# A written list of TensorE's work units, attention groups whose parts may stand apart, and new durations in a kernel's planner

## The chip, the cores and the metric

The kernel runs on one core of one Trainium2 chip. The metric is the device time of one execution, in microseconds (us); the numbers quoted are medians over runs of the same program.

## The reference, cut to what matters

Gated linear attention feeds a gMLP block. B = 4 batches, H = 8 heads, S = 768 steps, D = 48; the model width is 384 and the hidden width 1024.

```python
for t in range(S):                                   # per batch and head
    state = alpha[t][:, None] * state + k[t][:, None] * v[t][None, :]
    y[t] = q[t] @ state
x = y, heads side by side                            # (B, S, 384)
u, v = split(gelu_tanh(x @ w_in))                    # each (B, S, 512)
v_n = (v - mean(v)) / sqrt(var(v) + 1e-6) * g_ln
v_s = einsum('ts,bsd->btd', w_sg, v_n) + b_sg[:, None]
out = x + (u * v_s) @ w_out
```

## The kernel before, in words

The sequence is cut into 24 chunks of 128 steps, numbered through: six for each of the four batches, three for each half of a batch. The recurrence is done chunk by chunk with decays folded into q and k. On VectorE each chunk takes two scans (`scan`, L334, and `recip`, L352), the products of q and k with the decays (`q`, L344, and `k`, L362), the masked scores (`causal`, L476), and three small updates of the running state (`half`, L496; `add`, L501; `state`, L504).

TensorE's work comes in units with short names, which the text uses throughout:

- A **group** serves two chunks at once: it closes chunk o and opens chunk i, and is written o.i (a dash where one is missing). It has three parts. G o.i (`squares`) holds the scores of chunk i, the first half of chunk o's output and the two gains of the state; M o.i (`squares_more`) the second half of o's output; H o.i (`squares_end`) the last reads of the state, which need VectorE's `half` of chunk o, and the transposes of chunk i's k. All but the transposes are small products that use the array in quarters (64 by 64). M waits for `turn` of chunk o (L455), a tiny copy on ScalarE that orders two halves of a bank.
- V b c (`mlp_v`) projects chunk c of batch b to the half that is normalised. Behind it stand gelu on ScalarE (L565), moments on VectorE (L569, L573), a root and a shift on GpSimd (L577, L582), the normalisation on VectorE (L589) or ScalarE (L585), and the split into a high part `vh` (ScalarE, L593) and a low part `vl` (VectorE, L597).
- U b h d (`mlp_u`) projects half h of a batch, column block d; ScalarE's gelu follows (L616).
- P b h d (`mlp_spatial`) multiplies all six v's of a batch with `w_sg`. Behind it stand a scale (VectorE, L631), the gate (VectorE or GpSimd, L636), and the split into `gh` (ScalarE, L641) and `gl` (VectorE, L646).
- R b h k (`mlp_out`) multiplies with `w_out`; VectorE adds x (L676) and the result is stored.
- Early on there are short products that make the low parts of the weights (`low_pe`, named wv, wu and ws with a number). The weights `w_out` (wo) and the second half of `w_sg` are split on ScalarE, VectorE and GpSimd.

Between the close of a chunk and the first V or U that reads it stands a chain: ScalarE copies the output (`xf`, L518, and `y3`, L508), six small DMAs pack it (L521), ScalarE makes the high part (`xh`, L529), and VectorE or GpSimd the low part (`xl`, L533).

A planner written in the kernel sets the order in which the instructions are emitted, and each engine executes its own in that order. `Plan.add` registers a step with an engine, a duration in ns, the steps it comes after, and the buffers it takes. `Plan.issue` keeps an estimated clock for each engine and emits, again and again, the step that could start first; among TensorE's steps within 150 ns of each other the one due earliest goes first. The due times come from `units`, a list of TensorE's work with durations, summed up from 5000 ns. A step of TensorE may go ahead of the list's first open unit by at most four places. Buffers are few: three banks of PSUM for the products of the MLP (`mm`), two tiles `vg`, two tiles `g`, one pair `gh` and `gl`, three tiles kqv.

Of the kernel before, what the change touches and what calls it, by code (L numbers as in the profile page):

```python
# [18 lines left out]
B, H, S, D = 4, 8, 768, 48  # L19
# [19 lines left out]


class Plan:
# [5 lines left out]
    RATE = 280.0  # L47

# [40 lines left out]
    def issue(self, units, ahead):  # L89
# [7 lines left out]
        port = [0.0, None]  # L97
        dma = 0.0
        while left:
# [3 lines left out]
            for n, s in left.items():  # L103
# [23 lines left out]
                for e, lock, ns, fn in s["ways"]:  # L127
                    t1 = max(t, free[e])
# [15 lines left out]
            fn()  # L144
            free[e] = end - {"dve": 75, "act": 100, "pool": 45}.get(e, 0)
# [17 lines left out]
def tile_gla_gmlp(ctx: ExitStack, tc: tile.TileContext, aT, kqv, w_in, w_sgT, w_out, g_ln, b_sg, out):  # L163
# [391 lines left out]
    def mlp_v(x, t, c):  # L555
# [39 lines left out]
        def low_half():  # L595
# [13 lines left out]
    def mlp_u(x, t, d):  # L609
# [43 lines left out]

    def mlp_out(g, x, b, hf, kk):
# [119 lines left out]


    def group(o, i):
        i = i if i is not None and i < n else None
        name = ("G", o, i)
        if o is not None:
            o_at[o] = name  # L780
        if i is not None:
            s_at[i] = name
        first = [(name, 95 + SLOT * (2 if o is None else 3 if i is None else 5))]
        if o is not None:
            first.append((("M", o, i), 2 * SLOT))
        return first + [(("H", o, i), (0 if o is None else SLOT) + (0 if i is None else 530))]
# [5 lines left out]
    def u(b, hf, d):  # L792
        return [(("U", b, hf, d), 1560)]

    def p(b, hf, d):
        return [(("P", b, hf, d), 3120)]

    def v(b, c):
        return [(("V", b, c), 2080)]

    def r(b, hf):
        return [(("R", b, hf, kk), 2080) for kk in range(NK)]

    units += v(0, 3) + u(0, 0, 0) + v(0, 4) + u(0, 0, 1) + v(0, 5) + p(0, 0, 0) + group(None, NCH) + u(0, 0, 2)
    units += p(0, 0, 1) + u(0, 0, 3) + p(0, 0, 2) + group(NCH, NCH + 1) + u(0, 1, 0) + p(0, 0, 3)
    for b in range(B):
        g = (b + 1) * NCH
        if b > 0:
            units += group(g - 1, g) + v(b, 3) + u(b, 0, 0) + u(b, 0, 1) + u(b, 0, 2) + u(b, 0, 3) + v(b, 4) + v(b, 5)
            units += u(b, 1, 0) + (group(g, g + 1) if b < B - 1 else [])  # L810
            units += p(b, 0, 0) + p(b, 0, 1) + u(b, 1, 1) + p(b, 0, 2) + u(b, 1, 2) + p(b, 0, 3) + u(b, 1, 3)
        else:
            units += u(b, 1, 1) + u(b, 1, 2) + u(b, 1, 3)
        if b < B - 1:
            units += group(g + 1, g + 2) + r(b, 0) + p(b, 1, 0) + group(g + 2, g + 3)
            units += p(b, 1, 1) + p(b, 1, 2) + p(b, 1, 3) + group(g + 3, g + 4) + r(b, 1)
            units += v(b + 1, 0) + v(b + 1, 1) + group(g + 4, g + 5) + v(b + 1, 2)
        else:
            units += p(b, 1, 0) + r(b, 0) + p(b, 1, 1) + p(b, 1, 2) + p(b, 1, 3)
            units += [(("R", b, 1, kk, "begin"), 1560) for kk in range(2)] + r(b, 1)  # L820
# [14 lines left out]
    for name, p in pieces:  # L835
# [107 lines left out]
    for name, ns in units:  # L943
        if name[0] == "G":
# [12 lines left out]
            plan.add(name, "pe", ns, lambda o=o, i=i: squares(o, i), deps, takes, due=due[name])  # L957
        elif name[0] == "M":
# [3 lines left out]
                due=due[name], keen=500,  # L962
# [206 lines left out]
```

## Time and profile before

| | us |
|---|---|
| median of 3 runs (374.67 to 375.32) | 375.32 |
| the profiled execution, its own time | 377.39 |
| its span, from the first to the last instruction | 375.7 |
| TensorE busy in it | 347.4 (92%) |
| VectorE busy | 266.1 (71%) |
| ScalarE busy | 152.8 (41%) |
| GpSimd busy | 60.4 (16%) |

A profile names the engines PE (TensorE), PEld (its weight loads), DVE (VectorE), ACT (ScalarE), POOL (GpSimd) and SP (the engine that issues the DMAs). A row of a timeline has the start and the length in us, the engine, the line of the kernel, the operation and its tiles; in square brackets stands the idle time of the engine before it and what ended that. A row of a table by stretches has the stretch, its length, then for each engine the busy time and in brackets the number of instructions, then TensorE's granted clock as a share of full speed, and what the DMA engines did. Matmuls overlap in the records, so that the duration of one (0.34 us for a product of 384 columns) is longer than the distance to the next.

### The profile page before, as it was taken

The page shows a single profiled execution, that of the slowest core. Times are in us where ns is not written, and L with a number is a line of the kernel's source. Part 1 is how long each engine was busy: PE and PEld are TensorE (multiplying, and loading weights), DVE is VectorE, ACT ScalarE, POOL GpSimd, SP SyncE. Part 2 cuts the span into 40 slices and gives each one's busy share as a digit, 9 for nine tenths or more (in the row PEclk, how much of TensorE's full clock was granted, in tenths as well). Part 3 has the DMA queues.
Part 4 walks back from the last instruction along what each step waited for, and adds up shares of the span by engine and source line. Part 5 has one row for each costly group of instructions (what it writes and reads, how often), then busy time and mean ns, then how long its engine had stood idle before and what let it go on. Part 6 is the DMA issues. An engine that isn't in the chain of part 4 may idle for free.

```text
span 375.7 us, 10732 instructions
## 1 busy us (share of the span) xinstructions
PE 347.4 (92%) x4492; PEld 316.7 (84%) x4492; DVE 266.1 (71%) x527; ACT 152.8 (41%) x367; POOL 60.4 (16%) x103
## 2 busy tenths in 40 slices
PE   2795989999998799999999999899999999999993
PEld 2564868799998688989999998799999989799993
DVE  4799987899996957897564986787376646443351
ACT  3385476755433333673222435543223336311010
POOL 1002123413201120320101211420111113300000
PEclk9999699999999989999999999999999999999999
DMA  8855575125246133432043335130212020000102
GB/s 307 279 192 156 197 236 190 42 73 189 83 139 220 31 110 119 142 93 77 6 156 113 111 81 184 47 118 29 91 66 90 9 69 10 1 2 0 63 4 68
DMA packets 18856, 39.38 MB, mean 105 GB/s; under 512 B 3952, under 2 KB 10992, under 8 KB 18800
## 3 DMA queue, kind: packets, MB, share of 16 engines
q1 hardware_dynamic: 18800, 38.61, 31.9%
q8 instruction: 37, 0.61, 0.7%
q14 instruction: 19, 0.16, 0.1%
HBM read 32.70 MB, written 4.72 MB: 100 GB/s over the span
## 4 chain that ended last, share of the span: by engine, by line
PE 64%; DVE 14%; DMA 7%; ACT 4%; issue 4%; SPq 3%; POOL 2%; DVEq 0%; ACTq 0%; POOLq 0%
PE mm_s L552 7%; PE mm_s L550 7%; PE mm_s L551 7%; DMA xf<-y 3%; PE mm_u L550 3%; PE mm_u L551 3%; PE mm_u L552 3%; DMA kqv_t<-in_kqv 3%; PE mm_o L552 3%; PE mm_o L551 3%; PE mm_o L550 3%; PE y L390 3%; PE mm_v L550 3%; SPq L521 3%; PE mm_o L666 3%
## 5 line engine op out<-in xcount | busy, mean ns | idle before, releaser
L550 PE MATMUL mm_s<-ws_hi,vh 128*128 128x384 f32 x192 | 66.0, 344 | 1.4 <-ACT ws_hi L224 0.8
L552 PE MATMUL mm_s<-ws_hi,vl 128*128 128x384 f32 x192 | 65.2, 339 | 0.1
L551 PE MATMUL mm_s<-ws_lo,vh 128*128 128x384 f32 x192 | 65.1, 339 | 0.2 <-DVE ws_lo L227 0.2
L641 ACT CAST gh<-g 128x384 fp32r<-128x384 f32 x32 | 16.3, 512 | 58.4 <-DVE g L636 40.5
L631 DVE SCALAR_TENSOR_TENSOR g<-mm_s,g_col,b_bc 128x384 f32<-128x384 f32 x32 | 19.5, 608 | 27.0 <-PE mm_s L552 26.9
L550 PEld LDWEIGHTS mm_s<-ws_hi,vh 128*128 128x128 f32 x192 | 36.0, 188 | 2.6 <-ACT ws_hi L224 1.1
L551 PEld LDWEIGHTS mm_s<-ws_lo,vh 128*128 128x128 f32 x192 | 36.1, 188 | 0.6 <-DVE ws_lo L227 0.4
L552 PEld LDWEIGHTS mm_s<-ws_hi,vl 128*128 128x128 f32 x192 | 36.0, 188 | 0.6 <-DVE vl L597 0.6
L377 PE MATMUL sc<-kqv_t 64*64 64x64 f32 x768 | 27.8, 231 | 7.2 <-DVE kqv_t L362 4.5
L550 PE MATMUL mm_u<-xh,wi_hi 128*128 128x384 f32 x96 | 33.1, 345 | 0.0
L377 PEld LDWEIGHTS sc<-kqv_t 64*64 64x64 f32 x768 | 25.5, 146 | 8.3 <-DVE kqv_t L362 4.9
L551 PE MATMUL mm_u<-xl,wi_hi 128*128 128x384 f32 x96 | 32.4, 338 | 0.0
L552 PE MATMUL mm_u<-xh,wi_lo 128*128 128x384 f32 x96 | 32.4, 338 | 0.0
L550 PE MATMUL mm_v<-wi_hi,xh 128*128 128x512 f32 x72 | 30.8, 428 | 1.4 <-ACT u L616 1.4
L334 DVE TENSOR_TENSOR_SCAN pf<-a,floor 128x516 f32<-128x516 f32 x24 | 30.0, 1251 | 2.1 <-DMA a<-in_aT 1.9
L352 DVE TENSOR_TENSOR_SCAN pf<-a,floor 128x516 f32<-128x516 f32 x24 | 29.5, 1229 | 1.1 <-ACT pend L340 0.4
L551 PE MATMUL mm_v<-wi_lo,xh 128*128 128x512 f32 x72 | 28.9, 401 | 0.0
L390 PE MATMUL y<-at,kqv_t 64*64 64x64 f32 x768 | 22.7, 234 | 6.7 <-ACT y L508 3.6
L390 PEld LDWEIGHTS y<-at,kqv_t 64*64 64x64 f32 x768 | 16.9, 141 | 14.2 <-issue 5.1
L552 PE MATMUL mm_v<-wi_hi,xl 128*128 128x512 f32 x72 | 28.7, 399 | 0.0
L569 DVE BATCH_NORM_STATS2 stats<-vg 128x6 f32<-128x512 f32 x24 | 16.5, 688 | 14.1 <-ACT vg L565 14.1
L552 PE MATMUL mm_o<-gh,wo_lo 128*128 128x384 f32 (+1 forms) x77 | 25.5, 331 | 0.0
(116 smaller groups left out, 801.6 us busy)
## 6 DMA issues: line engine op xcount, KB each, us to landing
kqv_t<-in_kqv SPq DMA_DIRECT2D x24, 768.0 KB, 4.3
a<-in_aT SPq DMA_DIRECT2D x24, 258.5 KB, 2.7
out_x<-r SPq DMA_DIRECT2D x23, 192.0 KB, 1.9
raw<-in_w_in SPq DMA_DIRECT2D x8, 384.0 KB, 5.5
xf<-y SPq DMA_DIRECT2D x144, 8.0 KB, 2.4
raw<-in_w_out SPq DMA_DIRECT2D x4, 384.0 KB, 3.1
raw<-in_w_sgT SPq DMA_DIRECT2D x6, 192.0 KB, 2.5
raw_sg<-in_w_sgT SPq DMA_DIRECT2D x1, 768.0 KB
```

Source lines behind the costliest of these rows:

```text
L334: nc.vector.tensor_tensor_scan(pf.rearrange("p j t -> p (j t)"), s["a"][:, 0:NP * C1], floor.rearrange("p j t -> p (j t)"), initial=0.0, o ...
L352: nc.vector.tensor_tensor_scan(s["pf"].rearrange("p j t -> p (j t)")[:, ::-1], s["a"][:, NP * C1:0:-1], floor.rearrange("p j t -> p (j t)" ...
L377: lambda j=j, h=h: nc.tensor.matmul(sc[half(h), e, 64 * j:64 * j + 64], k[half(e), j, half(h)], q[half(e), j, half(h)], start=True, stop=True,
L390: lambda j=j: nc.tensor.matmul(y_of(y, j, e)[:, half(h)], v[half(h), j, half(e)], at[half(h), e, j], start=first and j < 2, stop=True, ski ...
L521: nc.sync.dma_start(xf[64 * e + D:64 * e + 64, kk, tsl], y3[64 * e + 16 * kk:64 * e + 16 * kk + 16, :])
L550: nc.tensor.matmul(o, lh, rh, start=(idx == 0), stop=False)
L551: nc.tensor.matmul(o, lh, rl, start=False, stop=False)
L552: nc.tensor.matmul(o, ll, rh, start=False, stop=(idx == n - 1))
L569: nc.vector.bn_stats(t["stats"], t["vg"])
L631: nc.vector.scalar_tensor_tensor(t["g"], t["o"], g_col[:, d:d + 1], b_bc[:, tsl], op0=ALU.mult, op1=ALU.add,)
L641: nc.scalar.copy(g["h"][:, d], t["g"])
L666: nc.tensor.matmul(t["o"], lh[:, d, sl], g[rh][:, d], start=False, stop=(rh == "l"))
```

## The change

Three things change; the arithmetic and the instructions themselves stay.

1. The list `units` was computed by loops in the code, with each group's G, M and H next to each other. It is now read from a string `ORDER` with one token for each unit, in another order, where M or H need not follow right behind its G. `Plan.issue` treats the list as before, with the same four places of freedom.
2. Durations that the planner uses are changed, most of them upwards by 2 to 25%; for instance `("pe", 3120, product)` becomes `("pe", 3180, product)` for P, and GpSimd's root goes from 800 to 860.
3. The planner adds 50 ns to its estimate where TensorE goes from full products to those in quarters, and 110 ns for the way back.

Since the planner chooses at some steps between engines by its estimate, some work changes its engine as well. By the emitted order, seven of the 24 normalisations go from VectorE to ScalarE, three low parts of the second half of `w_sg` and two of the k products go from VectorE to GpSimd, one `xl` as well, and four gates and two additions for `w_out` go from GpSimd to VectorE.

```diff
+ORDER = """
+    H-.0 G0.1 M0.1 G-.0 G1.2 H1.2 M1.2 H0.1 G2.3 M2.3 V00 H2.3 H3.4 G3.4 U000 V01 M3.4 H4.5 G4.5 V02 G5.- M4.5 M5.-
...
+    RATE = 280.0
+    SWITCH = {("full", "tiled"): 50, ("tiled", "full"): 110}
...
-                    t1 = max(t, free[e])
+                    t1 = max(t, free[e] + (self.SWITCH.get((mode, s["mode"][0]), 0) if e == "pe" else 0))
...
-            ("pe", 2080, product), ("act", 600, gelu), ("dve", 665, moments), ("dve", 150, mean),
-            ("pool", 800, root), ("pool", 220, shift), (("dve*", 540, norm), ("act", 760, norm_act)), ("act", 615, high),
-            ("dve*", 665, low_half),
+            ("pe", 2100, product), ("act", 600, gelu), ("dve", 690, moments), ("dve", 175, mean),
+            ("pool", 860, root), ("pool", 270, shift), (("dve*", 545, norm), ("act", 810, norm_act)), ("act", 615, high),
+            ("dve*", 680, low_half),
...
-    for i in range(NCH):
-        units += group(i - 1 if i > 0 else None, i)
-        units.append((("V", 0, i - 3), 2080)) if i > 2 else None
-    units += group(NCH - 1, None)
...
+    def unit(token):
+        kind, rest = token[0], token[1:]
+        if kind in "GMH":
+            o, i = (None if x == "-" else int(x) for x in rest.split("."))
+            name = (kind, o, i)
...
+    units = [unit(token) for token in ORDER.split()]
```

What this does to the order is shown at three places. The buffers in the names carry numbers that differ between the two programs; the lines of the changed kernel are 17 higher from the attention on.

The first place is TensorE behind group 7.8, which closes chunk 7. Before, U 0 1 3 follows (`mm_u`):

```order
L400 MATMUL y_1450<-kqv_t_821,s_c_98 64x64 x8
L400 MATMUL y_1450<-kqv_t_821,s_m_100 64x64 x8
L471 MATMUL tp_1530<-ident_78,kqv_t_922 128x128 x4
L550 MATMUL mm_u_1536<-xh_767,wi_hi_103 128x384
L551 MATMUL mm_u_1536<-xl_804,wi_hi_103 128x384
L552 MATMUL mm_u_1536<-xh_767,wi_lo_104 128x384
```

Now P 0 1 2 follows there (`mm_s`):

```order
L417 MATMUL y_1501<-kqv_t_877,s_c_98 64x64 x8
L417 MATMUL y_1501<-kqv_t_877,s_m_100 64x64 x8
L488 MATMUL tp_1576<-ident_78,kqv_t_967 128x128 x4
L567 MATMUL mm_s_1585<-ws_hi_107,vh_859 128x384
L568 MATMUL mm_s_1585<-ws_lo_108,vh_859 128x384
L569 MATMUL mm_s_1585<-ws_hi_107,vl_882 128x384
```

U 0 1 3 has moved forward to just ahead of the H that opens chunk 6. Taken together, up to the H of group 8.9 TensorE's order has P 0 1 0 and P 0 1 2 where it had R 0 0 0; all other units ahead of that point are the same ones.

The second place is VectorE ahead of `half` of chunk 9 (the last row), which H of group 9.10 needs. Before, these rows lead up to it, of them the scales, gates and low parts of P 0 1 1, 0 1 2 and 0 1 3 (`g`, `gl`):

```order
L631 SCALAR_TENSOR_TENSOR g_1821<-mm_s_1770,g_col_109,b_bc_110 128x384
L348 RECIPROCAL floor_91<-pf_1798 128x4
L636 TENSOR_TENSOR g_1821<-g_1821,u_1442 128x384
L646 TENSOR_TENSOR gl_1827<-g_1789,gh_1800 128x384
L646 TENSOR_TENSOR gl_1827<-g_1821,gh_1800 128x384
L631 SCALAR_TENSOR_TENSOR g_1850<-mm_s_1802,g_col_109,b_bc_110 128x384
L636 TENSOR_TENSOR g_1850<-g_1850,u_1498 128x384
L646 TENSOR_TENSOR gl_1827<-g_1850,gh_1800 128x384
L631 SCALAR_TENSOR_TENSOR g_1898<-mm_s_1831,g_col_109,b_bc_110 128x384
L496 TENSOR_TENSOR s_m_100<-s_c_98,dl0_1857 128x4x48
```

Now these do; the row with `kqv_t_1768` is `q` of chunk 11, the one with `r_1822` the addition behind R 0 0 0:

```order
L518 TENSOR_TENSOR s_m_100<-s_m_100,sc_1667 128x4x48
L379 TENSOR_TENSOR kqv_t_1604<-kqv_t_1604,pf_1661 128x512
L693 TENSOR_TENSOR r_1782<-mm_o_1647,xf_280 128x384
L521 TENSOR_TENSOR s_c_98<-s_m_100,pend_97 128x4x48
L351 SCALAR_TENSOR_TENSOR pf_1786<-a_1642,floor_91 128x516
L365 RECIPROCAL floor_91<-pf_1786 128x4
L361 TENSOR_TENSOR kqv_t_1768<-kqv_t_1768,pf_1786 128x512
L693 TENSOR_TENSOR r_1822<-mm_o_1789,xf_280 128x384
L369 SCALAR_TENSOR_TENSOR pf_1786<-a_1642,floor_91 128x516
L663 TENSOR_TENSOR gl_1870<-g_1474,gh_1819 128x384
L513 TENSOR_TENSOR s_m_100<-s_c_98,dl0_1829 128x4x48
```

Between `half` of chunk 8 and `half` of chunk 9 stood 27 instructions and stand 15.

The third place is ScalarE around `turn` of chunk 2 (`alo2`) and the copy `y3` of chunk 2, which has to be done before G of group 3.4 may write its output. Before:

```order
L455 COPY alo2_102<-alo_89 128x1
L340 COPY pend_97<-pf_499 128x4
L484 COPY kn_548<-tp_538 128x512
L518 COPY xf_281<-y_457 128x3x128
L366 ACTIVATE a_345,low_96<-a_345,alo_89 128x4x128
L529 CAST xh_431<-xf_281 128x3x128
L508 COPY y3_567<-y_457 128x128
```

Now:

```order
L472 COPY alo2_102<-alo_89 128x1
L252 CAST ws_lo_108<-mm_w_435 128x384
L252 CAST ws_lo_108<-mm_w_442 128x384
L357 COPY pend_97<-pf_454 128x4
L281 CAST wi_hi_103<-top_525 128x384
L501 COPY kn_549<-tp_535 128x512
L535 COPY xf_280<-y_458 128x3x128
L281 CAST wi_hi_103<-top_540 128x384
L383 ACTIVATE a_383,low_96<-a_383,alo_89 128x4x128
L298 CAST wi_lo_104<-mm_w_564 128x384
L525 COPY y3_585<-y_458 128x128
L546 CAST xh_438<-xf_280 128x3x128
```

The copy `y3` has passed ahead of `xh` of chunk 1, and a weight product's copy (`wi_lo_104<-mm_w_564`) now stands ahead of it: the products wv 2 and wv 3 have moved on TensorE from behind group 3.4 to ahead of it. In TensorE's emitted order three groups stand apart: V 0 0 is between G and M of 3.4, U 0 0 0 between G and M of 4.5, and P 0 0 2, P 0 0 0 and U 0 1 3 between G and H of -.6. All other groups are emitted with their parts next to each other.

More of the change, by code (lines that the diff above doesn't have):

```diff
@@ L53, in add @@
         self, name, eng, ns, fn, after=(), takes=(), lead={}, due=None, soon=None, nbytes=0, other=None, keen=0,
-        start=0.0,
+        start=0.0, mode=("full", "full"),
     ):
@@ L60, in add @@
             name=name, eng=eng.rstrip("*"), ns=ns, after=list(after), takes=list(takes), lead=lead, due=due, soon=soon,
-            nbytes=nbytes, keen=keen, start=start, ways=[(e.rstrip("*"), e in ("dve*", "pool"), c, f) for e, c, f in ways],
+            nbytes=nbytes, keen=keen, start=start, mode=mode, ways=[(e.rstrip("*"), e in ("dve*", "pool"), c, f) for e, c, f in ways],
         )
@@ L97, in issue @@
         port = [0.0, None]
+        mode = "full"
         dma = 0.0
@@ L144, in issue @@
             fn()
+            if e == "pe":
+                mode = s["mode"][1]
             free[e] = end - {"dve": 75, "act": 100, "pool": 45}.get(e, 0)
@@ L791, in tile_gla_gmlp @@
-    units += group(NCH - 1, None)
[L792 to L820, printed above, removed]
+    def unit(token):
[3 more added lines that the diff above has]
+            name = (kind, o, i)
+            if kind == "G":
+                if o is not None:
+                    o_at[o] = name
+                if i is not None:
+                    s_at[i] = name
+                return name, SLOT * (2 if o is None else 3 if i is None else 5)
+            if kind == "M":
+                return name, 2 * SLOT
+            return name, (0 if o is None else SLOT) + (0 if i is None else 420 if o is None else 530)
+        if kind == "B":
+            return ("R", B - 1, 1, int(rest), "begin"), 1590
+        if kind == "C":
+            return ("R", B - 1, 1, NK - 1, 0), 0
+        return (kind, *map(int, rest)), {"U": 1590, "P": 3180, "V": 2100, "R": 2120}[kind]
@@ L864, in tile_gla_gmlp @@
         last = at("low_pe") if on_pe else at("low")
-        plan.add(at("size"), "act", 510, p["size"], [at("load")], takes=[("mag", 2, [last])])
-        plan.add(at("clamp"), "dve*", 330, p["clamp"], [at("size")])
-        plan.add(at("shift"), "dve*", 330, p["shift"], [at("clamp")], takes=[("top", 2, [last])])
+        plan.add(at("size"), "act", 550, p["size"], [at("load")], takes=[("mag", 2, [last])])
+        plan.add(at("clamp"), "dve*", 345, p["clamp"], [at("size")])
+        plan.add(at("shift"), "dve*", 350, p["shift"], [at("clamp")], takes=[("top", 2, [last])])
         plan.add(at("sign"), "dve*", 550, p["sign"], [at("shift")])
         plan.add(at("high"), "act", 510, p["high"], [at("sign")])
-        plan.add(at("power"), "dve*", 330, p["power"], [at("sign")])
+        plan.add(at("power"), "dve*", 345, p["power"], [at("sign")])
         plan.add(at("rest"), "dve*", 550, p["rest"], [at("power")])
@@ L956, in tile_gla_gmlp @@
             takes.append(("sc", 1, users))
-            plan.add(name, "pe", ns, lambda o=o, i=i: squares(o, i), deps, takes, due=due[name])
+            plan.add(name, "pe", ns, lambda o=o, i=i: squares(o, i), deps, takes, due=due[name], mode=("tiled", "tiled"))
         elif name[0] == "M":
@@ L970, in tile_gla_gmlp @@
                 name, "pe", ns, lambda o=o, i=i: squares_end(o, i), deps, takes, lead={last: 215}, due=due[name], keen=500,
+                mode=("full" if o is None else "tiled", "tiled" if i is None else "full"),
             )
@@ L1050, in tile_gla_gmlp @@
                     first = r + ("begin",)
-                    plan.add(first, "pe", 1560, begin, deps[:ND - 1], [("mm", 3, [r + ("add",)])], due=due[first])
-                    plan.add(r, "pe", 520, end, deps + [first], due=due[r])
+                    plan.add(first, "pe", 1590, begin, deps[:ND - 1], [("mm", 3, [r + ("add",)])], due=due[first])
+                    plan.add(r, "pe", 530, end, deps + [first], due=due[r])
                 elif (b, hf) == (B - 1, 1):
```

36 lines of the change are left out of this document (17 added, 19 removed).

## The prediction

> **What bounds the kernel now.** I read the page's head and its costliest group first, then the table by stretches, then the waits and timelines of the stretches in which TensorE (PE) loses time.
>
> ```profile
> span 375.7 us, 10732 instructions
> PE 347.4 (92%) x4492; PEld 316.7 (84%) x4492; DVE 266.1 (71%) x527; ACT 152.8 (41%) x367; POOL 60.4 (16%) x103
> L550 PE MATMUL mm_s<-ws_hi,vh 128*128 128x384 f32 x192 | 66.0, 344 | 1.4 <-ACT ws_hi L224 0.8
> 8.34:54.00 45.66, 37.17 (x752) 28.60 (x754) 41.09 (x83) 27.03 (x72) 5.91 (x6) 0.93 0.65 212
> 54.00:112.00 58.00, 56.89 (x731) 50.84 (x720) 52.77 (x113) 32.49 (x76) 15.56 (x21) 1.00 0.40 128
> 112.00:135.00 23.00, 19.08 (x213) 17.12 (x212) 17.32 (x32) 8.19 (x21) 3.12 (x3) 0.93 0.40 121
> 135.00:239.00 104.00, 104.00 (x1454) 96.87 (x1453) 76.72 (x149) 42.66 (x104) 17.74 (x33) 1.00 0.34 106
> 239.00:244.00 5.00, 3.58 (x16) 2.68 (x15) 3.54 (x6) 3.27 (x8) 1.70 (x2) 1.00 0.12 42
> 244.00:324.00 80.00, 80.00 (x1077) 75.28 (x1077) 49.70 (x102) 29.43 (x70) 12.48 (x24) 1.00 0.18 57
> 324.00:330.00 6.00, 5.34 (x30) 4.42 (x29) 3.47 (x8) 1.63 (x3) 2.16 (x4) 1.00 0.00 1
> 330.00:376.00 46.00, 39.85 (x235) 39.68 (x233) 16.89 (x31) 5.28 (x11) 0.00 (x0) 0.98 0.08 28
> ```
>
> The group at the top, the first of the three products of P, shows how long one matmul lasts (0.344). In the table, after each stretch's length stand the busy times of PE, its weight loads, VectorE (DVE), ScalarE (ACT) and GpSimd, then PE's clock. From 135 to 324 PE pauses in one place only, for 1.42. An order can win there next to nothing. Up to 54 PE is idle for 8.5 and from 112 to 135 for 3.9, and up to 112 DVE is busy 91% of the time: there DVE decides. The rest is PE's own work, the same before and after.
>
> **Prices of the units**, from places where PE doesn't wait: P, U, V, R, a whole group, and a P with a group right behind it.
>
> ```profile
> 249.18:252.36 3.18, 3.18 (x20) 3.18 (x20) 2.27 (x6) 1.31 (x4) 0.36 (x1) 1.00 0.44 170
> 255.53:257.12 1.59, 1.59 (x10) 1.59 (x10) 1.59 (x4) 0.57 (x2) 0.00 (x0) 1.00 0.28 69
> 319.00:321.10 2.10, 2.10 (x10) 1.70 (x10) 0.00 (x0) 0.49 (x1) 0.00 (x0) 1.00 0.00 0
> 271.31:273.39 2.08, 2.08 (x13) 2.08 (x13) 1.84 (x3) 0.00 (x0) 0.00 (x0) 1.00 0.07 12
> 265.15:267.58 2.43, 2.43 (x133) 2.36 (x133) 1.66 (x3) 0.70 (x2) 1.00 (x1) 1.00 0.03 7
> 261.88:265.15 3.27, 3.27 (x20) 3.02 (x19) 0.56 (x1) 0.76 (x2) 0.00 (x0) 1.00 0.00 0
> ```
>
> Going from full products to quarters costs 0.09 (3.27 against 3.18); a split group adds one such way there and back. Groups 3.4 and 4.5 are split (-.6 was left and entered once in either order): 2 x 2 x 0.09 = 0.4, in a stretch where PE waits for DVE, so I book nothing; uncovered, it is 0.4. The Trainium skill (TensorEngine Tiling, Tiling Modes) says that changing the mode drains TensorE. It speaks against splitting; the trace agrees that a change costs, with 0.09. The page gives no price; were each drain as long as a whole matmul, 0.344, the four changes would come to 1.4.
>
> DVE's prices are these means, and the next instruction starts some 0.07 before the one ahead has run out (110.92 + 0.34 against 111.19, further below).
>
> ```profile
> L352 DVE TENSOR_TENSOR_SCAN pf<-a,floor 128x516 f32<-128x516 f32 x24 | 29.5, 1229 | 1.1 <-ACT pend L340 0.4
> L631 DVE SCALAR_TENSOR_TENSOR g<-mm_s,g_col,b_bc 128x384 f32<-128x384 f32 x32 | 19.5, 608 | 27.0 <-PE mm_s L552 26.9
> L476 DVE TENSOR_TENSOR at<-sc,mask 128x512 f32<-128x512 f32 x24 | 16.3, 678 | 4.6 <-PE y L390 3.2 <-PE sc L377 1.3
> L597 DVE TENSOR_TENSOR vl<-vg,vh 128x512 fp32r<-128x512 f32 x24 | 16.1, 679 | 6.1 <-ACT vh L593 6.1
> L676 DVE TENSOR_TENSOR r<-mm_o,xf 128x384 f32<-128x384 f32 x23 | 12.4, 548 | 12.9 <-PE mm_o L666 12.4 <-DMA out_x<-r 0.4
> L533 DVE TENSOR_TENSOR xl<-xf,xh 128x384 fp32r<-128x384 f32 x17 | 9.4, 552 | 4.8 <-ACT xh L529 4.8
> L255 DVE TENSOR_SCALAR top<-mag 128x384 int32<-128x384 int32 x12 | 4.0, 351 | 0.0
> ```
>
> **Step 1, up to chunk 5.**
>
> ```profile
> 37.83 0.71 PE L390 MATMUL y<-at,kqv_t 64*64 64x64 f32 x16 [3.57 <-ACT y L508]
> 38.00:44.00 6.00, 6.00 (x137) 5.30 (x138) 6.00 (x12) 2.66 (x7) 1.44 (x1) 0.57 0.40 113
> 56.02 0.41 PE L400 MATMUL y<-kqv_t,s_m 64*64 64x64 f32 x16
> ```
>
> G 3.4 waits 3.57 for ACT's `y3`, which stood behind `xh`, and behind that idle time PE's clock is 0.57 for 6 us. The new order takes `y3` from behind `xh` and puts the products wv 2 and 3 into the gap, but these need their own DVE steps, which end some 5 us of work behind `half` of chunk 2 (a reversed scan, a q product, three like xl and five short ones); PE idles about as long as before and the clock falls as before. I book 0. The Trainium skill (TensorE: Matmul & The Clock Gate, Part 1) says that the clock halves after an idle window of about 3.4 us; the row agrees. By that rule a gap cut below it would save up to 2.6 (6.0 x 0.43) of PE time.
>
> The gain comes behind it. Ahead of H 5.- (56.02) PE's list gains product wu 0, U 0 0 0 and V 0 2: at least 1.59 + 2.10 + about 1.1 = 4.8. Ahead of DVE's `half` of chunk 5 five instructions leave (a scan, a k product, an xl, two tiny ones: 2.7) and twelve come (five like xl, two vl, one moments, four short: 6.0); less seven overlaps, +2.8. So H 5.- comes 2.8 later with 4.8 more done: PE is 2.0 better off.
>
> **Step 2, up to chunk 8.**
>
> ```profile
> 110.92 0.34 DVE L496 TENSOR_TENSOR s_m<-s_c,dl 128x192 f32<-128x192 f32 x1
> 111.19 1.23 DVE L352 TENSOR_TENSOR_SCAN pf<-a,floor 128x516 f32<-128x516 f32 x1
> 111.32 0.46 PE L400 MATMUL y<-kqv_t,s_m 64*64 64x64 f32 x16
> ```
>
> DVE's `half` of chunk 8 ends at 111.26 and H 8.9 starts at 111.32: DVE decides. Ahead of this `half` DVE has 199 instructions in either order; eleven are exchanged, nine of some 0.55 and two scales of 0.61 for ten of 0.55 and a tiny one, +0.5. Ahead of H 8.9 PE has P 0 1 0 and P 0 1 2 for R 0 0 0: 2 x 3.18 - 2.08 = 4.28 more. If DVE's idle time up to here stays, H 8.9 stands at 111.9, and PE is 3.7 better off (2.0 of it from step 1).
>
> **Step 3, group 9.10.**
>
> ```profile
> 120.90 0.69 DVE L344 TENSOR_TENSOR kqv_t<-kqv_t,pf 128x512 f32<-128x512 f32 x1 [2.90 <-DMA kqv_t<-in_kqv]
> 131.40 0.34 DVE L496 TENSOR_TENSOR s_m<-s_c,dl 128x192 f32<-128x192 f32 x1
> 130.51 0.46 PE L390 MATMUL y<-at,kqv_t 64*64 64x64 f32 x16 [2.26 <-ACT alo L455]
> 131.80 0.61 PE L400 MATMUL y<-kqv_t,s_m 64*64 64x64 f32 x16 [0.60 <-DVE s_m L496]
> 133.10:136.31 3.21, 3.21 (x11) 2.55 (x10) 1.18 (x3) 1.21 (x4) 0.00 (x0) 0.65 0.77 248
> ```
>
> M waits 2.26 for `turn` and H 0.60 for `half` of chunk 9, which is done 20.5 after that of chunk 8. V 1 0 then takes 3.21, not 2.10, at a clock of 0.65. Now 15 DVE instructions stand between the two halves: three scans or reversed scans would be 3.7, three additions 1.65, q, k and scores 2.1, a gl 0.58, five small 1.1, 9.1 in all and less overlaps 8.0. With `half` of chunk 8 at 111.3 + 0.5, that of chunk 9 ends at 120.1, or at 123.0 if the 2.90 for chunk 11's kqv come back whole (it is loaded once H 8.9 has freed its buffer, as before). PE reaches H 9.10 at 111.9 + 3.18 + 2.08 + 2.10 (P, R, V) + 2.43 = 121.7. I take 122.3, between the two, not 131.80: 9.5 earlier. V 1 0 is done by then and P 0 1 1 is not: 3.18 - 2.10 = 1.1 goes off. Of that H's own wait of 0.6 goes too, and V's slow clock (1.1). Together 10.1.
>
> **Step 4, the two later stalls, and what takes their place.**
>
> ```profile
> 243.01 0.50 PE L550 MATMUL mm_v<-wi_hi,xh 128*128 128x512 f32 x1 [1.42 <-ACT u L616]
> 324.98:329.44 4.46, 3.80 (x21) 3.16 (x20) 2.13 (x6) 1.14 (x3) 1.66 (x3) 1.00 0.01 2
> 230.23 0.66 PE L471 MATMUL tp<-ident,kqv_t 128*128 128x128 f32 x4
> 238.93 0.56 DVE L533 TENSOR_TENSOR xl<-xf,xh 128x384 fp32r<-128x384 f32 x1 [0.45 <-ACT xh L529]
> ```
>
> V 2 4 waited 1.42 behind a crowd of gelus; the new list spreads V's and U's, -1.4. P 3 0 0 takes 4.46 for 3.18 since the last `vl` is late; now U 3 0 3, U 3 0 0 and two R stand between V 3 4 and it (7.3 us), -1.2. New: U and V stand closer behind the chunks that they read. The chain for chunk 17 took 9.3 from its transposes (230.23) to the end of `xl` (239.49); V 2 2 now has 10, V 2 4 11, V 0 5 10 behind their chunks' H. Seven more normalisations on ACT lie in its 59% of idle time. These places cost between 0 and 6; I take 1.5, since most of the rows have a little to spare.
>
> Sum: 10.1 + 1.4 + 1.2 - 1.5 = 11.2. The profiled span of 375.7 becomes 364.5. The median lies 0.4 below that span: 364.1. The tail behind the last matmul keeps its order.
>
> **Rivals.** (a) A smaller gain: DVE's idle time up to chunk 9 grows by 3 to 8 (it had, by the two rows of the table that end at 112, 9.8 in all), or the new close reads take 5 to 6 and the idle time 1 to 4 more: 367.5 to 374.5. For it: every place in the new list has 0 to 2 us to spare; against: DVE has less work to do ahead of chunk 9. (b) Slower: DVE's `xl`, at the head of a queue that executes in order, waits for the packing DMAs.
>
> ```profile
> 60.32 0.56 DVE L533 TENSOR_TENSOR xl<-xf,xh 128x384 fp32r<-128x384 f32 x1 [1.20 <-ACT xh L529]
> ```
>
> Chunk 4's waits 1.20 before. Four such (chunks 1, 3, 4, 5) stand in DVE's new order up to V 0 5. Everything behind is moved by each us waited; from 2.8 more for each the gain is gone, and at 4 the time is 380. Against it: each stands behind 9 to 11 us of other work. (c) The list doesn't matter, since DVE's total hardly changes and it stays the bound up to the second batch: within 0.2%. Against it: DVE is busy 17.32 of 23.00 from 112 to 135. (d) More gain: the clock doesn't fall at 38 and no close read waits: 357 to 360.
>
> **How the numbers follow.** 0.2%, 0.75 us, is about what a measurement tells from no change. Forecast (360 to 367.5) 0.56, (a) 0.25, (b) 0.08, (c) 0.04, (d) 0.07. Faster is the first, (a) and (d): 0.88; same 0.04; slower 0.08. The range leaves out (b), (c), the slowest fifth of (a) and the lower half of (d), 0.2 in all: 358.5 to 372.5. It takes in the bounds of step 3 (H 9.10 from 121.7 to 123.3) and of step 4 (0 to 6).
>
> **What would show it.** H 8.9 near 112 and H 9.10 near 122 in PE's timeline; no wait of M 9.10 for `alo`; PE without pauses from 125 on, but for waits under 1 us at V 2 2, V 2 4 and V 3 5; P 3 0 0 in 3.2. The forecast is wrong if H 8.9 comes after 115, if DVE waits over 2 us for `xh` in the first 70 us, or if PE loses over 5 us behind 135.

## The result, and the profile after

The changed kernel takes 368.1 us (median; 365.55 to 370.98), the kernel before 375.2 on the same chips. The ratio is 0.986, with a 95% interval of 0.983 to 0.989; it leaves out executions of the kernel before that stood over 1.5% above its fastest (the profiled one, with 377.39, stood there too), and so gives 5.2 us (375.2 x 0.0139) where the medians give 7.1. The forecast was 364.1 and a gain of 11.2: the direction is right and the time lies in the range, but the gain is only 0.47 (by the ratio) to 0.63 (by the medians) of what was forecast.

The page's head and the table by the same stretches as before, of the profiled execution of after (367.87 us):

```profile
span 366.1 us, 10776 instructions
PE 343.3 (94%) x4492; PEld 315.0 (86%) x4492; DVE 263.3 (72%) x520; ACT 157.7 (43%) x374; POOL 61.3 (17%) x103
8.34:54.00 45.66, 38.56 (x747) 28.87 (x748) 38.87 (x82) 28.66 (x73) 4.71 (x8) 0.96 0.67 215
54.00:112.00 58.00, 56.62 (x614) 51.21 (x614) 53.85 (x110) 33.33 (x78) 17.15 (x20) 1.00 0.42 130
112.00:135.00 23.00, 21.55 (x472) 20.25 (x472) 21.38 (x40) 10.64 (x29) 7.80 (x9) 1.00 0.46 138
135.00:239.00 104.00, 104.00 (x1334) 97.21 (x1333) 78.43 (x153) 47.88 (x113) 21.49 (x36) 1.00 0.34 104
239.00:244.00 5.00, 5.00 (x95) 4.75 (x96) 2.43 (x5) 0.70 (x2) 0.00 (x0) 1.00 0.00 0
244.00:324.00 80.00, 80.00 (x1028) 75.83 (x1020) 49.25 (x99) 28.74 (x68) 8.50 (x19) 1.00 0.17 53
324.00:330.00 6.00, 6.00 (x36) 6.00 (x35) 3.20 (x6) 0.98 (x2) 0.00 (x0) 1.00 0.01 3
330.00:366.10 36.10, 30.09 (x180) 29.64 (x178) 11.30 (x22) 3.94 (x8) 0.00 (x0) 0.96 0.10 35
```

Behind 135 us PE no longer pauses until its last work is done: both late stalls are gone, and no close read put another in their place. From 112 to 135 PE is busy 21.55 of 23.00 (19.08 before). Up to 112 little changed, and DVE is still the fuller engine there. The timeline around the two places on which the forecast hung:

```profile
114.94 0.34 DVE L513 TENSOR_TENSOR s_m<-s_c,dl 128x192 f32<-128x192 f32 x1
115.33 0.29 PE L417 MATMUL y<-kqv_t,s_m 64*64 64x64 f32 x4 [1.45 <-DVE s_m L513]
121.02 0.69 DVE L361 TENSOR_TENSOR kqv_t<-kqv_t,pf 128x512 f32<-128x512 f32 x1 [0.52 <-DMA kqv_t<-in_kqv]
124.69 0.35 DVE L513 TENSOR_TENSOR s_m<-s_c,dl 128x192 f32<-128x192 f32 x1 [0.83 <-PE dl L428]
125.39 0.30 PE L417 MATMUL y<-kqv_t,s_m 64*64 64x64 f32 x8
```

DVE's `half` of chunk 8 begins 4.0 later than before (114.94 against 110.92), and PE, in H 8.9, waits 1.45 for it: H 8.9 comes behind 115, which the prediction named as a sign that it is wrong. `half` of chunk 9 then comes 9.75 behind it, not 20.5, and the wait for `alo` is gone.

To set whole executions side by side, I took for each of PE's units the time to the start of the next one, less the usual time of its kind (the 20th percentile over this case's profiles), and summed these losses by where the unit starts. The span less the loss is 339.6 to 340.1 in every row, so the work is the same and the loss is what differs. The first four rows are the two kernels, each with a second profile; the others are the experiments below (us):

```
                          0-60  60-115  115-140  140-end   all    span
before                   20.23    4.30     5.44     5.95  35.92  375.68
before, second profile   20.44    4.30     2.87     5.90  33.51  373.11
after                    18.60    4.03     0.55     2.97  26.16  366.08
after, second profile    18.65    3.62     0.92     2.85  26.05  366.19
list_alone               20.21    4.12     2.63     4.56  31.52  371.22
durations_alone          24.39    3.62     2.62     5.08  35.72  375.41
no_switch                16.72    6.85     6.54     3.62  33.73  373.78
groups_whole             22.58    7.20     4.52     5.88  40.18  379.92
list_to_H89              17.37    3.88     0.46     5.31  27.03  366.85
list_from_batch1         25.95    4.05     3.74    11.68  45.42  385.31
pool_one_input_before    19.96    3.63     3.03     4.89  31.51  371.49
pool_one_input_after     17.64    1.59     0.51     2.90  22.65  362.37
lows_on_vector           17.09    4.35     0.57     2.95  24.97  364.62
after_q_first            19.60    3.58     1.61     4.61  29.40  369.20
no_switch_q_first        15.67    7.00     5.72     3.00  31.38  371.05
before_q_first           19.89    5.04     0.95     4.54  30.42  370.18
```

### The profile page after: what moved, and what is told of

The parts are those of the page before. It is cut to its first block, busy times and chain, and to the rows that moved or that the text cites. A ratio compares the mean times of both kernels' runs of the same rounds, so it can differ in the third digit from the quotient of the medians.

```text
span 366.1 us, 10776 instructions
## 1 busy us (share of the span) xinstructions
PE 343.3 (94%) x4492; PEld 315.0 (86%) x4492; DVE 263.3 (72%) x520; ACT 157.7 (43%) x374; POOL 61.3 (17%) x103
## 4 chain that ended last, share of the span: by engine, by line
PE 77%; DVE 12%; issue 3%; DMA 2%; POOL 2%; ACT 2%; SPq 0%; DVEq 0%; ACTq 0%; POOLq 0%
PE mm_s L567 8%; PE mm_s L569 8%; PE mm_s L568 8%; PE mm_v L567 4%; PE mm_v L569 4%; PE mm_v L568 4%; PE mm_u L567 4%; PE mm_u L568 4%; PE mm_u L569 4%; PE y L407 3%; PE mm_o L569 3%; PE mm_o L568 3%; PE mm_o L567 3%; PE mm_o L683 3%; PE tp L488 3%
## 5 line engine op out<-in xcount | busy, mean ns | idle before, releaser
L567 PE MATMUL mm_v<-wi_hi,xh 128*128 128x512 f32 x72 | 29.8, 414 | 0.0
L594 POOL TENSOR_SCALAR rstd<-mv 128x1 f32<-128x1 f32 x24 | 8.3, 345 | 128.0 <-DVE mv L590 116.8
L693 DVE TENSOR_TENSOR r<-mm_o,xf 128x384 f32<-128x384 f32 x23 | 12.6, 550 | 21.2 <-PE mm_o L683 21.0
L567 PE MATMUL mm_o<-gh,wo_hi 128*128 128x384 f32 (+1 forms) x77 | 25.6, 333 | 0.0
L568 PE MATMUL mm_o<-gl,wo_hi 128*128 128x384 f32 (+1 forms) x77 | 25.6, 332 | 0.0
```

What stands on the lines that cost most here:

```text
L567: nc.tensor.matmul(o, lh, rh, start=(idx == 0), stop=False)
L568: nc.tensor.matmul(o, lh, rl, start=False, stop=False)
L693: nc.vector.tensor_tensor(t["r"], t["o"], x["xf"][:, kk], op=ALU.add)
```

## The experiments

The kernel before ran beside each set of experiments, with medians from 372.7 to 375.2 us. Medians of different sets therefore differ by up to 2.5 us without a cause in the kernel; the ratios, each to the kernel before of its own set, are what compares.

**Which part of the change carries it.** Four kernels took parts of it.

*list_alone* is the kernel before with the written list alone; *durations_alone* is the changed kernel with the old list:

```diff
 list_alone:       before.py, the loops over group, u, p, v, r replaced by
+    units = [unit(token) for token in ORDER.split()]
 durations_alone:  after.py, with the old loops back in place of that line
```

> The kernel before with the new list of TensorE's units, and the old durations and no price for a change of tiling in the planner. Theory: the list carries the gain, since the rows that got better are TensorE's (the group 9.10 without its wait for alo, no stall behind 125 us); 366 to 370 us, ratio to the kernel before 0.98 to 0.99. Rival: the corrected durations set VectorE's order, and VectorE is what TensorE waits for ahead of 115 us, so the list alone gains less than half: 372 to 375 us.

> The changed kernel with the old list, so that only the planner's durations and its price for a change of tiling differ from the kernel before. Theory (the list carries the gain): 373 to 377 us, within 0.5% of the kernel before. Rival (the durations carry it, by VectorE's order): 369 to 372 us.

Measured: 371.4 us for the list alone (ratio 0.995, 0.991 to 0.998) and 378.7 for the durations alone (1.010, 1.004 to 1.015). Neither theory holds, nor does a rival. The two parts add up to nothing (-3.8 and +3.5 by medians), together they give -7.1. In the timeline of durations_alone a place where it loses shows, and in the table of its stretches from 32 us on:

```profile
40.39 0.49 PE L407 MATMUL y<-at,kqv_t 64*64 64x64 f32 x8 [6.56 <-ACT y L525]
32.00:36.00 4.00, 1.57 (x56) 1.13 (x48) 4.00 (x10) 1.19 (x4) 0.00 (x0) 0.93 0.29 77
36.00:40.00 4.00, 0.00 (x0) 0.00 (x0) 4.00 (x11) 2.25 (x6) 0.16 (x1) 0.50 0.72 254
40.00:44.00 4.00, 3.61 (x128) 3.50 (x128) 4.00 (x7) 1.34 (x5) 0.92 (x1) 0.50 0.05 10
```

With the corrected durations the planner hands DVE other work first, and G 3.4 waits 6.56 us, not 3.57, with PE's clock at half speed behind it. The list puts two weight products and, further on, V 0 0 between a group's parts into this stretch; in the changed kernel no wait there is longer than 2.18. The list alone, with the old durations, already brings `half` of chunk 9 close behind that of chunk 8 (116.64), and M 9.10 and H 9.10 don't wait:

```profile
126.37 0.35 DVE L509 TENSOR_TENSOR s_m<-s_c,dl 128x192 f32<-128x192 f32 x1 [0.34 <-PE dl L424]
```

*list_to_H89* and *list_from_batch1* split the list in two:

```diff
 list_to_H89:       after.py
+    cut = ORDER.split().index("V10")
+    units = units[:cut] + [x for x in old if x[0] not in taken]
 list_from_batch1:  the old order through batch 0's R, then ORDER's rows for the rest
```

> The changed kernel with the new list up to the third row that holds R000 (through group 8.9's opening), and the old order of the rest; durations as in the changed kernel. By the two traces H 8.9 came only some 0.3 us better than before, so that the theory (the gain up to there was lost to VectorE, and comes only from group 9.10 on) gives 373 to 376 us. Rival (what is gained is already there at H 8.9, and the old order would keep it): 369 to 372 us.

> The changed kernel with the old list through batch 0's products R, and the new order for all that follows. In the two profiled executions 4.3 us of the 9.6 were gained behind H 9.10. Theory: the new order behind there takes the stalls of V24 and P300 away in every execution: 370 to 372 us. Rival: these 4 us were mostly one unlucky execution of the kernel before (its profiled time stood 2.2 us above its median), and the gain lies ahead of 125 us: 373 to 376 us.

Measured: 369.9 us (ratio 0.989, 0.983 to 0.995) for the head, against the theory and with its rival; 384.5 (1.026, 1.019 to 1.033) for the tail, which neither expected. The head with the old order behind it already has a loss of 0.46 from 115 to 140: there it doesn't matter what the list says behind H 8.9. It has lost 5.31 behind 140, like before (5.95), and P 3 0 0 takes 4.18 again:

```profile
316.38:320.56 4.18, 3.81 (x21) 3.17 (x20) 2.02 (x5) 1.73 (x4) 1.31 (x3) 1.00 0.01 2
```

So the new tail is worth the other 2.3 of the profile, and 1.8 of the medians, a difference that lies inside the interval. The tail behind the old head says nothing on its own worth: at the seam P 1 0 2 has to wait 2.58, and 5.7 us more than before are lost behind 140 (in an execution 2.5 above this kernel's median).

**Parts of a group apart.** In *groups_whole* PE takes nothing else between a group's G and its H:

```diff
+                if opened and s["ways"][0][0] == "pe":
+                    if n[1:] != opened or n[0] not in ("M", "H"):
+                        continue
```

> The changed kernel with one rule more in the planner: between a group's G and its H TensorE takes nothing else, so that a group's three parts stand together as before. Theory: the parts that stand apart hide the wait of M for alo (2.26 us in the group 9.10 before) and of H for half (0.6 us each in several groups of before); without them the groups 3.4, 4.5, 8.9 and some later ones wait again: 370 to 374 us. Rival: the durations already order VectorE and ScalarE so that these waits are short, and TensorE waits as long in sum wherever the parts stand: 367 to 369 us.

Measured: 377.6 us, ratio 1.009 (1.005 to 1.013): 9.5 above the changed kernel (8.5 by the ratios), past the theory's own end. The profiled execution was 4 us above this median, so its rows give places, not sizes. At M 4.5, behind whose G the changed kernel does U 0 0 0, PE stands first; later R waits for a low part of `w_out`, and DVE's q of chunk 11 for its load:

```profile
55.87 0.26 PE L422 MATMUL y<-kqv_t,s_c 64*64 64x64 f32 x1 [4.02 <-issue]
114.08 0.69 PE L574 MATMUL mm_o<-gh,wo_lo 128*128 128x384 f32 x1 [2.58 <-DVE wo_lo L310]
51.00:56.00 5.00, 0.98 (x63) 0.84 (x58) 2.92 (x10) 0.51 (x1) 2.57 (x6) 0.89 0.47 165
56.00:60.00 4.00, 4.00 (x30) 3.88 (x30) 2.85 (x6) 2.20 (x6) 0.00 (x0) 0.50 0.59 191
129.66 0.69 DVE L366 TENSOR_TENSOR kqv_t<-kqv_t,pf 128x512 f32<-128x512 f32 x1 [3.80 <-DMA kqv_t<-in_kqv]
```

At M 4.5 PE does 0.98 us of work in five, and its clock then halves. The loss from 60 to 140 is 11.7, against 4.6 in the changed kernel. But the waits that the theory names don't show: up to 140 us no M waits for `alo` and no H for `half` by more than 0.1, and the row of the longest wait names no releaser. So the time is shown and the cause isn't. The list was found for parts that may stand apart, so this is what it loses without them, not what another list for whole groups would take.

**Why `half` of chunk 8 came late.** DVE's idle time from 18 us to this instruction had grown by only 1.1 (7.6 against 6.5). Its instructions were longer: set against the median of their own kind, they were stretched by 6.0 in sum, against 2.9 before, and every stretched one lies beside a large two-input operation of GpSimd, of which there are 11 in that time, and 8 before. The 1.1 of idle time and 3.1 more of stretch account for the 4.0. From the timeline of after, ahead of `half`, with one more stretched row (0.35 is usual):

```profile
111.90 1.30 POOL L550 TENSOR_TENSOR xl<-xf,xh 128x384 fp32r<-128x384 f32 x1 [7.72 <-ACT xh L546]
112.32 1.29 DVE L653 TENSOR_TENSOR g<-g,u 128x384 f32<-128x384 f32 x1
113.16 1.30 POOL L653 TENSOR_TENSOR g<-g,u 128x384 f32<-128x384 f32 x1
113.54 1.48 DVE L361 TENSOR_TENSOR kqv_t<-kqv_t,pf 128x512 f32<-128x512 f32 x1
90.95 1.05 DVE L272 TENSOR_SCALAR top<-mag 128x384 int32<-128x384 int32 x1
```

DVE's gate takes 1.29, usually 0.56, and its q product 1.48, usually 0.69; they end 0.41 and 0.56 after GpSimd's operations (113.20, 114.46), as if most of each had begun only then. The Trainium skill (SBUF — State Buffer, Who interferes with whom) says that a DVE instruction with two SBUF inputs contends with a GpSimd instruction that reads SBUF, for a pair of ports that is an exclusive lock. The gate and the q product agree. The row at 90.95 has one tensor input and is stretched too (GpSimd works from 90.79 to 91.79), so two inputs aren't the whole condition. *pool_one_input_after* and *pool_one_input_before* make GpSimd's operations shorter and change no order; they leave one input out of the arithmetic:

```diff
-        eng.tensor_tensor(xl[:, :, tsl], xf[:, :, tsl], xh[:, :, tsl].bitcast(F32), op=ALU.subtract)
+        if eng is nc.gpsimd:
+            eng.tensor_copy(xl[:, :, tsl], xh[:, :, tsl].bitcast(F32))
+        else: ...            # and so for ws_lo, wo_lo, top, the gates and k
```

> The changed kernel with each large two-input operation of GpSimd (xl, the low halves of the spatial and output weights, the gates that GpSimd takes, k) made a copy of one of its inputs, the one that comes last; order and waits as they were, results not the reference's. Theory: ten VectorE instructions stretched by 0.2 to 0.8 us (6.0 us in sum up to half 8) each lie beside such an operation of GpSimd, which holds VectorE off by its second input; as copies they don't, the stretch sum falls below 1.5 us, H 8.9 comes at 110 to 112.5 us instead of 115.3, and the time is 363.5 to 366.5 us. Rival: any large operation of GpSimd holds VectorE so: stretch sum above 3 us, 367 to 369 us.

> The kernel before with the same edit (GpSimd's two-input operations as copies of one input; results not the reference's). Theory: its stretch sum up to half 8 was 2.9 us, so that it gains half as much as the changed kernel does from the same edit: 372.5 to 374 us. Rival: no change, 374.5 to 376 us.

Measured: 364.8 us (ratio 0.974, 0.969 to 0.979, where the changed kernel has 0.986) and 373.2 (0.994, 0.990 to 0.999), both as the theory had it, and the stretch sums fell to 1.2 and 0.2. GpSimd's groups from 18 to 115 us of after, then the same two from 18 to 112 with copies, and the timeline with copies:

```profile
L550 POOL TENSOR_TENSOR xl<-xf,xh 128x384 fp32r<-128x384 f32 x4 | 5.5, 1381 | 56.8 <-ACT xh L546 29.6 <-DMA a<-in_aT 27.3
L653 POOL TENSOR_TENSOR g<-g,u 128x384 f32<-128x384 f32 x2 | 3.2, 1610 | 4.2 <-DVE g L648 4.2
```
```profile
L563 POOL CAST xl<-xh 128x384 fp32r<-128x384 f32 x4 | 3.5, 870 | 58.6 <-ACT xh L558 58.6
L669 POOL COPY g<-g 128x384 f32<-128x384 f32 x2 | 1.9, 964 | 4.1 <-DVE g L663 4.1
111.15 0.35 DVE L525 TENSOR_TENSOR s_m<-s_c,dl 128x192 f32<-128x192 f32 x1 [0.25 <-PE dl L440]
121.86 0.35 PE L429 MATMUL y<-kqv_t,s_m 64*64 64x64 f32 x12
```

A copy lasts some 0.5 us less. Where it still meets DVE, the stretch is at most 0.3 where it was up to 0.8, so what counts is how long GpSimd holds on; the expectation's words on the second input say too much. `half` of chunk 8 now starts at 111.15, as it did before (110.47 in the kernel before with copies), and H 8.9 and H 9.10 stand at 111.85 and 121.86, where the forecast had 111.9 and 122.3.

*lows_on_vector* asks the question from the other side: is such an operation cheaper on DVE itself?

```diff
+        if i < NCH + 3:
+            on_vector(("xl", i))                 # takes GpSimd out of a step's two ways
-                    at("low"), "pool", 1000, lambda p=p: p["low_half"](nc.gpsimd), [at("high")],
-                    other=("dve*", 545, lambda p=p: p["low_half"](nc.vector)),
+                    at("low"), "dve*", 545, lambda p=p: p["low_half"](nc.vector), [at("high")],
```

> The changed kernel, and up to batch 0's end the large two-input operations that the planner may give to GpSimd (xl 0 to 8, the low halves of the weights, batch 0's gates) go to VectorE alone. Theory (such an operation costs VectorE as much on GpSimd as on itself: 11 of them ahead of half 8 went with 6.0 us of stretch, 0.54 us each, against 0.48 to 0.55 us on VectorE): within 1 us of the changed kernel, 367 to 369 us, half 8 at 113 to 116 us. Rival (GpSimd takes real work off VectorE): half 8 after 118 us and 371 to 374 us.

Measured: 366.5 us (365.54 to 367.43), ratio 0.979 (0.973 to 0.985), a little better than the theory had it. DVE's stretch is nil, and `half` of chunk 8 starts earlier though DVE does all the work:

```profile
112.18 0.37 DVE L513 TENSOR_TENSOR s_m<-s_c,dl 128x192 f32<-128x192 f32 x1
```

This is the fastest version with the whole arithmetic, but its interval meets that of the changed kernel, so the 1.6 us between them aren't shown.

**The clock in the gap at 36 to 44 us.** *gap_filled* puts 28 small matmuls by zeros where PE waited 2.18; *after_again* is the changed kernel once more, unchanged:

```diff
+            for _ in range(fill):
+                nc.tensor.matmul(o[:, 0:P], nothing, mask, start=False, stop=False)
             nc.tensor.matmul(o, ident, t["mag"], start=False, stop=True)
```

> The changed kernel with 28 matmuls of 128x128 by a tile of zeros ahead of the last matmul of wv2's product, where TensorE waited 2.18 us for VectorE; they add zero to the sum. Theory (the granted clock fell to 0.86 and 0.71 in 36 to 44 us because of that wait, and in the run with the list up to H 8.9, with the same rows, it did not): the clock stays at 1.00 up to 52 us, G 3.4 takes 1.3 us instead of 2.1, 366 to 367.3 us and a narrower spread. Rival: VectorE bounds the stretch up to 60 us anyway, so the time stays, 367.5 to 368.5 us.

> The changed kernel once more, for a second profile. Theory: the granted clock in 36 to 44 us is what differs between its executions, and no stall returns behind 125 us; span 363.5 to 368 us, and if the clock stays at 1.00 in 36 to 44 us, 363.5 to 365.5 us. Rival: stalls behind 125 us return in some executions, up to 2 us.

Measured: 367.9 us (ratio 0.982, 0.975 to 0.989), the rival's time. The same stretch in after, in its second profile, in list_to_H89 (PE has the same rows up to 42 us) and in gap_filled:

```profile
36.00:40.00 4.00, 2.57 (x7) 1.47 (x7) 4.00 (x10) 1.97 (x5) 0.00 (x0) 0.86 0.85 269
40.00:44.00 4.00, 4.00 (x87) 3.21 (x87) 3.08 (x8) 1.77 (x5) 0.00 (x0) 0.71 0.49 183
```
```profile
36.00:40.00 4.00, 2.40 (x5) 1.49 (x5) 4.00 (x10) 1.63 (x6) 0.00 (x0) 0.64 0.77 265
```
```profile
36.00:40.00 4.00, 2.54 (x21) 1.47 (x24) 4.00 (x10) 2.02 (x6) 0.00 (x0) 1.00 0.89 282
```
```profile
36.00:40.00 4.00, 3.40 (x36) 2.53 (x34) 4.00 (x10) 2.37 (x7) 0.00 (x0) 1.00 0.66 213
```

Filled, the clock stays up, and no gain shows in the time. The second profile of after has its span at 366.2 with a fallen clock, and no stall behind 140. But the profile of gap_filled is no clean comparison: its first q product on DVE waited 1.84 for its load, not 0.36, and DVE ran 1.4 behind the changed kernel's up to 40 us and still 1.0 behind from 44 to 50. And DVE doesn't set the pace alone there, since in after it waits for PE where the clock is low:

```profile
42.10 0.35 DVE L513 TENSOR_TENSOR s_m<-s_c,dl 128x192 f32<-128x192 f32 x1 [0.92 <-PE dl L428]
41.13 0.34 DVE L513 TENSOR_TENSOR s_m<-s_c,dl 128x192 f32<-128x192 f32 x1
```

The second row is the same instruction in list_to_H89, whose DVE has the same order up to `half` of chunk 8: level with after at 40 us, it is 1.0 ahead here and 1.5 ahead at 54. So the fallen clock goes with a loss of about 1 us at this place; whether any of it reaches the median isn't shown.

**The planner's price for a change of tiling.** *no_switch* empties it:

```diff
-    SWITCH = {("full", "tiled"): 50, ("tiled", "full"): 110}
+    SWITCH = {}
```

> The changed kernel without the planner's price for a change of tiling; the corrected durations and the new list stay. Theory: a change of tiling was measured at 0.09 us, so that the price moves only a few choices: 367 to 370 us. Rival: the price is what spares the waits (the list with old durations and without it took 371.4 us): 370.5 to 372.5 us.

Measured: 375.5 us, ratio 1.007 (1.003 to 1.011): the whole gain is gone, more than either theory said. The price itself is small, but without it about 100 of DVE's 520 rows stand elsewhere. The rows where it loses:

```profile
115.79 0.39 PE L407 MATMUL y<-at,kqv_t 64*64 64x64 f32 x4 [2.96 <-ACT alo L472]
123.47 0.69 DVE L361 TENSOR_TENSOR kqv_t<-kqv_t,pf 128x512 f32<-128x512 f32 x1 [5.31 <-DMA kqv_t<-in_kqv]
137.24 0.34 PE L417 MATMUL y<-kqv_t,s_m 64*64 64x64 f32 x8 [1.92 <-DVE s_m L513]
```

The product q of chunk 11 stands in DVE's queue 12 steps behind `half` of chunk 8 in the changed kernel, and 5 here. Its load starts only as H 8.9 lets go of a buffer, and takes 4.7 us there and 6.0 here, so a DVE that is early stands still, ahead of `half` of chunk 9. Splitting the load, q first, tests that, in four kernels (before, no_switch, after, lows_on_vector); *before_again* is the kernel before once more, unchanged:

```diff
-        nc.sync.dma_start(kqv_t, kqv[i])
+        nc.sync.dma_start(kqv_t[:, 1], kqv[i][:, 1])
+        nc.sync.dma_start(kqv_t[:, 0:3:2], kqv[i][:, 0:3:2])
```

> The kernel before once more, for a second profile. Theory (its stalls are set by the order): G 3.4 waits 3 to 4 us, M 9.10 2 to 2.6 us for alo, V24 1.2 to 1.6 us, P300 takes over 4 us, all of them again; span 373 to 376 us. Rival (chance of one execution): the waits behind 125 us are under half of these, span 371 to 373 us.

> The kernel before with the same split of the load. Its q11 stood 2.90 and 1.87 us in two executions whose spans differ by 2.6 us. Theory (M 9.10 waits for what stands behind q11 in VectorE's order): 372 to 373.5 us, and M 9.10's wait under 1 us. Rival: 374 to 375.5 us.

> The kernel without the planner's price for a change of tiling (375.5 us), with the same split of the load. Its q11 stood 5.31 us, only four instructions behind half 8. Theory (that wait carries much of its loss): it falls to some 3 us, 372.5 to 374 us. Rival (its loss lies in the late wo_lo at R001 and M 8.9's 2.96 us, ahead of q11): 375 to 376 us.

> The changed kernel with each chunk's load of k, q and v (768 KB) split in two: q first, then k and v. Theory: q11 stood 0.52 and 2.19 us in two executions for that load, issued as H 8.9 ended and 4.7 to 5.4 us on its way; a third of it should land 2 us sooner (192 KB stores take 2.0 us), so that q11 doesn't wait and H 9.10 comes 0.5 to 2 us sooner: 365.5 to 367.5 us. Rival (VectorE's other work sets half 9, or the second transfer's issue and bytes cost as much): 367.5 to 369 us.

> The kernel with the large two-input operations of batch 0 on VectorE alone (366.5 us), with the same split of the load. Its q11 did not wait (13 instructions behind half 8). Theory: nothing to gain, 366 to 367 us. Rival: earlier q elsewhere, 364.5 to 365.8 us.

Measured: the second profile of before has G 3.4's 3.67, V 2 4's 1.17 and P 3 0 0's 4.46 again, but less of what follows the load:

```profile
112.00:135.00 23.00, 20.14 (x242) 18.51 (x233) 17.55 (x33) 8.56 (x22) 3.64 (x3) 1.00 0.43 137
120.03 0.69 DVE L344 TENSOR_TENSOR kqv_t<-kqv_t,pf 128x512 f32<-128x512 f32 x1 [1.87 <-DMA kqv_t<-in_kqv]
129.65 0.46 PE L390 MATMUL y<-at,kqv_t 64*64 64x64 f32 x16 [1.54 <-ACT alo L455]
```

With q first, q11 waits 0.52 in the kernel before, M 9.10 not at all for `alo`, and the loss from 115 to 140 is 0.95. So that stall came from the load, as far as one profile shows it. The time, 372.5, is what the theory had, but the ratio, 1.000 (0.996 to 1.004), doesn't part it from no change. no_switch_q_first takes 375.1 (1.005, 1.001 to 1.008): q11's wait falls to 2.37, and M 8.9 still waits 2.98 for `alo`, so the load explains little of that kernel's loss. after_q_first takes 369.2 (0.989, 0.985 to 0.993) and lows_q_first 366.9 (0.982, 0.978 to 0.986): q11 waits for nothing and no time is won, since in the changed kernel `half` of chunk 9 waits 0.83 for PE's own `dl` at its end. In the second profile of after q11 waited 2.19, and `half` of chunk 9 came 10.42 behind that of chunk 8, only 0.7 more than in the first.

## Why the prediction was half right

By medians the forecast missed 4.0 us (368.1 against 364.1). 1.6 is in the span (366.1 against 364.5). The other 2.4 is in "the median lies 0.4 below that span": after's median lies 2.0 above its profiled span, as its profiled execution does with 1.8. In the profiled execution of before, 1.7 lay around the span too; that execution was 2.1 above the median, and its excess was in a stall that the sum then counted as won.

- *Step 1* (2.0 up to chunk 5): H 5.- reads `half` at 59.50, 3.5 later and not 2.8; with the 4.8 more done PE is 1.3 better off. G 3.4's wait and the fallen clock were booked as before; the clock fell less than before, and still goes with about 1 us of DVE's time against list_to_H89.
- *Step 2* (H 8.9 at 111.9, 3.7 better off with step 1) is the step that failed. H 8.9 came at 115.33: 4.0 later with 4.28 more done, so PE was 0.3 better off there. "If DVE's idle time up to here stays" was nearly met (+1.1); what failed is the price of DVE's work, taken as so many instructions at their means (+0.5). Beside GpSimd's operations DVE's instructions last longer: 0.54 us for each of the 11 operations (6.0 in sum, 3.1 more than before), as much as DVE's own 0.55. So work that the planner gives to GpSimd, which the sum counted as gone from DVE, still holds it. With GpSimd's operations shortened, H 8.9 stands at 111.85, as forecast.
- *Step 3* (6.4 more; H 9.10 at 122.3). The mechanism is right: `half` of chunk 9 follows chunk 8's by 9.75, not 20.5, and M 9.10 doesn't wait. With the copies H 9.10 stands at 121.86. In the profiled executions the size fits as well: from H 8.9 to H 9.10 PE takes 10.06, not 20.48, with 5.36 less to do, which is 5.1, and V 1 0's slow clock (1.1) is gone. The sum of 6.4 counts H 9.10's wait of 0.6 twice, since 131.80 already stands behind it; without that the forecast gain is 10.6. But much of the stall was chance of that execution: from 115 to 140 it lost 5.4 and the second one 2.9, of which 4.9 and 2.0 went. The list does this without the corrected durations too (list_alone: 9.74), and in durations_alone M 9.10 doesn't wait either, so this place doesn't need both.
- *Step 4* (1.1): 3.0 behind 140 us. The two stalls went as priced; the 1.5 for close reads was nothing. That hides part of step 2's miss, which is why the span missed by only 1.6: luck.
- "A split group ... I book nothing": the gain of splitting wasn't booked either, and with whole groups the same list and durations take 9.5 more by medians. The waits of M and H that split groups were thought to hide don't show there, so the reason is open.
- The rivals: the time fell into (a)'s range, by another cause than (a) names. (b) didn't come, DVE's waits for `xh` stay below 1 us. Of (d)'s conditions, the clock that doesn't fall was met in gap_filled without its gain.

What stays open: why PE stands 3 us at M 8.9 in no_switch (for ScalarE's `alo`) and 4 us at M 4.5 in groups_whole (the row names no releaser). Neither chain was followed to its start, so why the tiling price and the split groups are worth so much is not shown.

## What to carry to other kernels

An order tuned with its planner is one object: the list alone and the durations alone were worth -4 and +4 us here, and leaving out the tiling price or the split groups cost the whole gain, so a part's price can't be read from the others' sum. Work moved from VectorE to GpSimd wasn't off VectorE here: look for VectorE instructions above their usual length beside GpSimd's, which idle time doesn't show, and price the move with that. And before a stall is booked as a gain, ask whether it recurs: a second profile of the kernel before would have taken 2.6 off this forecast.

## What the runs showed of the hardware

A GpSimd operation of 128x384 with two inputs (1.0 to 1.9 us) stretched a VectorE instruction started under it by up to 0.8 us, and by 0.54 on the mean of 11 operations, as much as VectorE takes to do one (0.55). A one-input copy in its place (0.5 to 1.4 us) stretched one by at most 0.3. PE's clock fell to 0.86 and 0.64 in 36 to 40 us with no single wait longer than 2.18, and with the same rows of PE stayed at 1.00 in list_to_H89 and in no_switch (wait 2.17). The rule that the prediction cites from the Trainium skill (TensorE: Matmul & The Clock Gate, Part 1), an idle window of some 3.4 us, doesn't describe that: here a shorter wait went with a fallen clock in some executions and not in others.
